# GpSimd in place of VectorE for the low parts of h and x in a split-precision feed-forward kernel

## The chip, the cores and the metric

The kernel runs on one core of one Trainium2 chip. The metric is device time in microseconds (us) of one execution, the median of several. The engines are named as the profile names them: PE is TensorE (matmuls), PEld its weight loads, DVE is VectorE, ACT is ScalarE, POOL is GpSimd and SP is SyncE, which issues all the DMAs here.

## What is computed

A gated linear attention runs over 4 batches, 8 heads, 768 steps and a head size of 48. Its output, laid out as 3072 tokens by 384, goes through a feed-forward layer with a squared ReLU (384 to 2048 to 384). The part of the reference that matters:

```python
for t in range(S):
    state = alpha[:, :, t, :, None] * state + np.einsum('bhd,bhe->bhde', k[:, :, t], v[:, :, t])
    y[:, :, t] = np.einsum('bhd,bhde->bhe', q[:, :, t], state)
x = y.transpose(0, 2, 1, 3).reshape(B * S, H * D)
h = np.maximum(x @ w_in, 0.0)
out = h * h @ w_out
```

## The kernel before

The attention is cut into 24 blocks (4 batches times 6 chunks of 128 steps). Four blocks make one group of 512 tokens, so there are six groups, 0 to 5. While the attention of one group is computed, the feed-forward layer of the group before it runs on TensorE; the two are woven together in program order.

For each group the feed-forward layer has an *input pass* (x times w_in, 16 tiles of h, each 128 features by 512 tokens) and an *output pass* (h squared times w_out, summed over the 16 tiles for four blocks of 128 tokens). Group 0's input pass and parts of the first output passes work with plain 32-bit matmuls. All else uses a faster matmul type with fewer bits (`fp32r`), and makes up for the lost bits by splitting every operand into parts:

- the *high part* `a` is a rounded copy of the tile, made by ScalarE (L596, tiles `ha`, `hx`, `xa`),
- the *low part* `l` is the tile minus its high part (L597, through the helper `combine`, so that the profile shows it under L547; tiles `hl`, `hx`, `xl`),
- the *difference* `d` is the low part minus 2^-12 times the high part, made by VectorE (L600, tiles `hd`, `xd`).

The weights are split in the same way (`wb`, `wl`, `wd`, L549 to L573), once, and the parts are kept in DRAM and streamed back for later groups. The product is then a sum of three matmul series: high with high (`a`, `b`), low with low (`l`, `l`), and difference with difference (`d`, `d`). In the input pass (L622) they are called for each tile j of h: the three matmuls with `xa`, the three with `xl`, and two tiles later the three with `xd`. In the output pass (L701) `out_x` first goes through the tiles n of h, and for each through four blocks: `ha` with `wb`, then `hl` with `wl`, eight matmuls a tile. Only after that `out_y` goes through the differences `hd` with `wd`.

h itself is made from the sums in PSUM by ScalarE and VectorE (L636 to L660); its square on VectorE is L651 or an L547 `hid<-hid`.

The order on every engine is the program order: the pool runs under a manual schedule, and `weave` (L923) places the attention's steps and the splits between the feed-forward units by costs and due times that are written in the table `AT`. In groups 2 to 5 the first three tiles of h are split already during the input pass (`AHEAD`). The other thirteen are split in the output pass, up to six tiles ahead of TensorE (`ahead`); the four named `hx` use tiles of the pool `raw`, in which x and its parts lie, the rest tiles of the pool `two` (22 buffers). Group 1 splits eight tiles of h, since the rest of its output pass is plain; group 0 splits four.

The low part of x is made in `split_x` (L609), three tiles of 128x512 in each of groups 1 to 5, ahead of the group's input pass.

GpSimd does the setting of zeros and of constants in the first 6 us. Later its queue holds only twelve empty instructions (`passed`, L456): one for each part of the attention's output products. [...]

The function around the change:

Of the kernel before, what the change touches and what calls it, by code (L numbers as in the profile page):

```python
# [9 lines left out]
FP32 = mybir.dt.float32  # L10
# [3 lines left out]
ALU = mybir.AluOpType  # L14
# [11 lines left out]
def kernel(  # L26
# [12 lines left out]
    nc = tc.nc  # L39
# [505 lines left out]
    def combine(steps):  # L545
        for o, x, op, z in steps:
            nc.vector.tensor_tensor(out=o, in0=x, in1=z, op=op)  # L547
# [46 lines left out]

    def split_to(a, l, x):
        nc.scalar.activation(out=a, in_=x, func=AF.Copy, scale=NEAR)  # L596
        combine(((l, x, ALU.subtract, a.bitcast(FP32)),))  # L597

    def diff_to(d, a, l):
        nc.vector.scalar_tensor_tensor(  # L600
# [8 lines left out]
    def split_x(g, kk):  # L609
        if kk == 0:  # L610
            x_parts["x"], x_parts["a"], x_parts["l"] = xT.pop(g), raw_r("xa"), raw_r("xl")
        split_to(x_parts["a"][:, kk], x_parts["l"][:, kk], x_parts["x"][kk])
# [68 lines left out]
    def split_h(n, i):  # L681
        r = i % (AHEAD + MORE)
        if r < AHEAD:
            a, l = two_k("ha", FP32R), two_k("hl", FP32R)
        else:
            if i == AHEAD:
                extra[:] = [raw_r("hx") for _ in range(3)]
            x = 2 * (r - AHEAD)
            a, l = (extra[y // 3][:, y % 3] for y in (x, x + 1))
        split_to(a, l, hid.pop(n))  # L690
        h_parts[n] = a, l
# [338 lines left out]
```

## Time and profile before

| what | value |
|---|---|
| three timed runs | 522.41, 522.62 and 522.86 us; median 522.62 |
| span of the profiled execution | 520.6 us from its first to its last instruction |
| what the median has beyond that span | 2.0 us |
| VectorE, 128x512 subtraction of `hl`, `hx`, `xl` | 40, 36 and 15 of them, mean 688, 685 and 688 ns |
| VectorE, difference `hd`, `xd` (L600) | 76 and 15, mean 692 and 685 ns |
| ScalarE, high part `ha`, `hx`, `xa` (L596) | 40, 36 and 15, mean 639, 618 and 640 ns |
| granted TensorE clock | 1.00 over the whole span |

The profile comes from one execution, whose own time beside its span was not taken down; the three runs are other executions. In a group's line the text behind the count is the busy time in us, the mean of one in ns, and then the engine's idle time ahead of the group with what ended it. A line of the timeline has the start, the length, the engine, the line of the code and the tiles, written as output<-inputs. PE's busy time is modelled, and its matmuls overlap, so that a busy TensorE isn't always one at its peak. Spans on POOL are rough.

### The profile page before, as it was taken

What the parts mean: (1) busy time and instruction counts of PE and PEld (TensorE: products, weight loads), DVE (VectorE), ACT (ScalarE), POOL (GpSimd) and SP (SyncE); (2) the same over time, 40 slices, a digit from 0 to 9 for tenths busy, and PEclk for the clock granted to TensorE, in tenths of its full rate; (3) what the DMA queues carried; (4) which work ended last, traced back from release to release, by engine and by line L of the source; (5) the groups of instructions that cost most, each with busy time, mean ns of one, the idle gap of its engine ahead of it and who ended that gap; (6) DMA issues with size and microseconds to landing.
All of it is one profiled execution on the core that took longest, in us unless ns stands there. A gap on an engine that the chain in (4) does not pass through costs nothing.

```text
span 520.6 us, 12925 instructions
## 1 busy us (share of the span) xinstructions
PE 510.8 (98%) x5276; PEld 418.2 (80%) x5276; DVE 366.0 (70%) x631; ACT 313.0 (60%) x650; POOL 5.4 (1%) x29
## 2 busy tenths in 40 slices
PE   7989999999999999999999999999999999999997
PEld 4754455668887668988899988899988899988997
DVE  4798989979978787867597476587465476363861
ACT  4668785677888594575963275963275763164620
POOL 4000000000000000000000000000000000000000
PEclk9999999999999999999999999999999999999999
DMA  9999687244686787898884788964673534898201
GB/s 161 209 278 213 196 240 218 60 114 176 224 200 196 195 246 198 264 317 206 195 248 148 251 246 198 230 187 150 231 255 126 179 126 151 268 340 293 70 0 62
DMA packets 140995, 102.36 MB, mean 197 GB/s; under 512 B 111476, under 2 KB 114568, under 8 KB 140936
## 3 DMA queue, kind: packets, MB, share of 16 engines
q1 hardware_dynamic: 140936, 101.53, 68.3%
q8 instruction: 42, 0.69, 0.6%
q14 instruction: 17, 0.14, 0.1%
HBM read 84.18 MB, written 17.33 MB: 195 GB/s over the span
## 4 chain that ended last, share of the span: by engine, by line
PE 93%; DVE 2%; SPq 2%; DMA 1%; issue 1%; POOL 1%; ACT 0%; POOLq 0%; DVEq 0%
PE o L701 41%; PE h L622 32%; PE h L805 7%; PE y L352 4%; PE T L482 2%; PE sckv L372 2%; PE sckv L395 2%; PE cs L265 1%; DMA qk_lent<-in_q_dram 1%; SPq L303 1%; SPq L109 1%; PE cs L268 1%; PE cs L269 1%; DVE x L515 0%; DVE w_in L182 0%
## 5 line engine op out<-in xcount | busy, mean ns | idle before, releaser
L622 PE MATMUL h<-xa,wb 128*128 128x512 f32 x240 | 68.2, 392 | 0.0
L622 PE MATMUL h<-xl,wl 128*128 128x512 f32 x240 | 67.9, 391 | 0.0
L622 PE MATMUL h<-xd,wd 128*128 128x512 f32 x240 | 67.3, 396 | 0.0
L515 ACT COPY x<-y 32x256 f32<-32x256 f32 (+2 forms) x132 | 47.2, 366 | 25.4 <-PE y L352 20.1
L547 DVE TENSOR_TENSOR hid<-h,hid 128x512 f32<-128x512 f32 x40 | 27.6, 689 | 45.5 <-PE h L622 45.4
L701 PE MATMUL o<-wb,ha 128*128 128x384 f32 x160 | 54.6, 342 | 0.0
L701 PE MATMUL o<-w_out,hid 128*128 128x384 f32 x160 | 54.0, 491 | 0.0
L701 PE MATMUL o<-wd,hd 128*128 128x384 f32 x304 | 53.8, 334 | 0.0
L701 PE MATMUL o<-wl,hl 128*128 128x384 f32 x160 | 53.5, 335 | 0.0
L639 ACT ACTIVATE h<-h 128x512 f32<-128x512 f32 x40 | 23.3, 582 | 49.7 <-PE h L622 49.7
L622 PEld LDWEIGHTS h<-xl,wl 128*128 128x128 f32 x240 | 45.1, 188 | 10.0 <-DVE xl L547 0.4
L701 PEld LDWEIGHTS o<-wd,hd 128*128 128x128 f32 x304 | 52.7, 188 | 0.3 <-DVE osb L737 0.3
L622 PEld LDWEIGHTS h<-xa,wb 128*128 128x128 f32 x240 | 44.6, 188 | 9.3 <-ACT xa L596 0.2
L622 PEld LDWEIGHTS h<-xd,wd 128*128 128x128 f32 x240 | 44.2, 188 | 9.2
L701 PE MATMUL o<-wb,hx 128*128 128x384 f32 x144 | 48.7, 338 | 0.0
L701 PE MATMUL o<-wl,hx 128*128 128x384 f32 x144 | 48.1, 334 | 0.0
L701 PEld LDWEIGHTS o<-w_out,hid 128*128 128x128 f32 x160 | 29.8, 190 | 19.3
L637 ACT ACTIVATE hid<-h 128x512 f32<-128x512 f32 x40 | 24.0, 600 | 34.6 <-PE h L622 34.5
L805 PE MATMUL h<-x,w_in 128*128 128x512 f32 (+1 forms) x108 | 43.6, 552 | 1.2 <-ACT x L515 1.2
L596 ACT ACTIVATE ha<-hid 128x512 fp32r<-128x512 f32 x40 | 25.6, 639 | 25.5 <-DVE hx L547 16.1
L805 PEld LDWEIGHTS h<-x,w_in 128*128 128x128 f32 x108 | 19.9, 190 | 21.1 <-issue 17.2
L547 DVE TENSOR_TENSOR hl<-hid,ha 128x512 fp32r<-128x512 f32 x40 | 27.5, 688 | 10.1 <-ACT ha L596 10.1
(114 smaller groups left out, 879.7 us busy)
## 6 DMA issues: line engine op xcount, KB each, us to landing
wd<-do SPq DMA_DIRECT2D x36, 384.0 KB, 3.7
wl<-lo SPq DMA_DIRECT2D x34, 384.0 KB, 4.0
wl<-li SPq DMA_DIRECT2D x32, 384.0 KB, 3.5
wd<-di SPq DMA_DIRECT2D x32, 384.0 KB, 3.9
raw<-in_moe_w_in_dram SPq DMA_DIRECT2D x8, 768.0 KB, 5.6
raw<-in_moe_w_out_dram SPq DMA_DIRECT2D x8, 768.0 KB, 5.6
v_in<-in_v_dram SPq DMA_DIRECT2D x24, 192.0 KB, 4.7
out_dram<-osb SPq DMA_DIRECT2D x24, 192.0 KB, 1.9
```

Source lines behind the costliest of these rows:

```text
L352: ins = nc.tensor.matmul(out=ys[e][64 * half : 64 * half + D + G * e, m % 2, p // 2, t], lhsT=lhsT, rhs=rhs, start=(half, e) not in seen, ...
L372: nc.tensor.matmul(out=ps[e][HALF[h], 0, p, :], lhsT=ks[rows, p, HALF[h]], rhs=qs[rows, p, HALF[h]], start=True, stop=True, skip_group_che ...
L395: nc.tensor.matmul(out=ps[h][64 * e : 64 * (e + 1), 1, p, G:64], lhsT=tile_of("k", n)[HALF[h], 2 * p + e, :], rhs=tiles["v"][n % NV][HALF[ ...
L482: nc.tensor.transpose(out=ps[h][:, i, p, :], in_=rows[HALF[h], 128 * p : 128 * (p + 1)], identity=ident[HALF[h], HALF[h]],)
L515: copy(out=x[kk][to : to + m, t : t + 2], in_=blk[n]["y"][e][r : r + m, :, p // 2],)
L547: nc.vector.tensor_tensor(out=o, in0=x, in1=z, op=op)
L596: nc.scalar.activation(out=a, in_=x, func=AF.Copy, scale=NEAR)
L622: nc.tensor.matmul(out=acc["h", j], lhsT=here[w, "i", p][:, kk, jj * 128 : (jj + 1) * 128], rhs=x_parts[x][:, kk], start=start and kk == 0 ...
L637: nc.scalar.activation(out=hid[j], in_=x, func=AF.Copy, scale=E)
L639: nc.scalar.activation(out=x, in_=x, func=AF.Copy, scale=1.0 + E)
L701: nc.tensor.matmul(out=acc[t][:, 0:DM], lhsT=lhs[:, t * C : (t + 1) * C], rhs=rhs, start=start, stop=stop, skip_group_check=True,)
L805: nc.tensor.matmul(out=ps, lhsT=w[:, kk, c0 : c0 + 128], rhs=xT[g][kk][:, cols], start=(kk == 0), stop=(kk == KM - 1),)
```

## The change

One line: the subtraction in `split_to`, which `split_x` and `split_h` call, is issued on GpSimd. Its operands, its place in the program and the buffers stay. The high part stays on ScalarE, the difference on VectorE, and the weights' subtractions (L561, L572) stay on VectorE.

```diff
     def split_to(a, l, x):
         nc.scalar.activation(out=a, in_=x, func=AF.Copy, scale=NEAR)
-        combine(((l, x, ALU.subtract, a.bitcast(FP32)),))
+        nc.gpsimd.tensor_tensor(out=l, in0=x, in1=a.bitcast(FP32), op=ALU.subtract)
```

76 subtractions of h and 15 of x, all 128x512, change their engine. In the program the calls of `split_to` stand behind those of `ga` that come earlier in the woven order, and so do the subtractions behind the empty instructions of L456 in GpSimd's queue.

## The prediction

> **What bounds the kernel.** First the busy times and the chain of work that ended last, on the page of before.
>
> ```profile
> PE 510.8 (98%) x5276; PEld 418.2 (80%) x5276; DVE 366.0 (70%) x631; ACT 313.0 (60%) x650; POOL 5.4 (1%) x29
> ...
> PE 93%; DVE 2%; SPq 2%; DMA 1%; issue 1%; POOL 1%; ACT 0%; POOLq 0%; DVEq 0%
> ```
>
> TensorE sets the time. Of its 9.8 us idle nearly all lies at the two ends; the stretches that I summed from 60 to 505.6 us (all but 212 to 217) show 0.96 us idle at 203 us, put down to "issue", and 0.04 us more. So relieving VectorE can win almost nothing, and what counts is whether TensorE must wait for a low part. The groups, kept apart by shape, give the prices:
>
> ```profile
> L547 DVE TENSOR_TENSOR hl<-hid,ha 128x512 fp32r<-128x512 f32 x40 | 27.5, 688 | 10.1 <-ACT ha L596 10.1
> L257 DVE TENSOR_TENSOR lo<-a_in,hi 128x384 fp32r<-128x384 f32 x16 | 8.9, 559 | 0.6
> L256 DVE CAST hi<-a_in 128x384 fp32r<-128x384 f32 x16 | 5.7, 355 | 6.5 <-ACT a_in L244 6.5
> L208 POOL COPY halves_mask<-causal 64x64 f32<-64x64 f32 x2 | 0.5, 234 | 0.1
> L204 POOL CAST causal_r<-causal 128x128 fp32r<-128x128 f32 x1 | 0.3, 291 | 0.1
> ```
>
> The margin is read from the timeline of the last group (VectorE alone), where the output pass begins and ends:
>
> ```profile
> 484.48 0.68 DVE L547 TENSOR_TENSOR hid<-hid 128x512 f32<-128x512 f32 x1
> 485.08 0.69 DVE L547 TENSOR_TENSOR hx<-hid,hx 128x512 fp32r<-128x512 f32 x1
> 485.87 0.69 DVE L600 SCALAR_TENSOR_TENSOR hd<-hx 128x512 fp32r<-128x512 f32 x1
> 486.48 0.68 DVE L547 TENSOR_TENSOR hx<-hid,hx 128x512 fp32r<-128x512 f32 x1
> ...
> 502.19 0.69 DVE L547 TENSOR_TENSOR hl<-hid,ha 128x512 fp32r<-128x512 f32 x1
> ```
>
> and TensorE's weight loads in the same stretch, the first that reads the low part of h tile 3 and the first that reads that of tile 15:
>
> ```profile
> 487.79 0.19 PEld L701 LDWEIGHTS o<-wl,hx 128*128 128x128 f32 x1
> ...
> 504.43 0.19 PEld L701 LDWEIGHTS o<-wl,hl 128*128 128x128 f32 x1
> ```
>
> Tile 3 is ready at 485.77, 2.0 us ahead of its load; tile 15 at 502.88, 1.6 us ahead. TensorE takes (504.43 - 487.79) / 12 = 1.39 us a tile (8 matmuls), VectorE a subtraction and a difference (`hd`, L600), some 1.40 us from start to start. Both run level, and the margin is thin. The same reading, tile 15: 1.9 us in groups 2 and 4 (281.55 to 282.23 against a load at 284.09; 435.77 to 436.46 against 438.45), 2.8 in group 3. Group 1 has only five such tiles, with 3.6 to 9.6 us, and group 0 four with 1.9 to 6.2.
>
> The low part of x has no margin in group 1. VectorE's three subtractions, and the weight load that waits for the third:
>
> ```profile
> 126.95 1.90 DVE L547 TENSOR_TENSOR xl<-x,xa 128x512 fp32r<-128x512 f32 x3 [0.92 <-ACT xa L596]
> ...
> 128.90 0.19 PEld L622 LDWEIGHTS h<-xl,wl 128*128 128x128 f32 x1 [0.36 <-DVE xl L547]
> ```
>
> In groups 2 to 5 `xl` is ready 2.7 to 9.5 us ahead.
>
> **Removed and added.** 91 subtractions of 128x512 (76 of h, 15 of x) leave VectorE's queue, 62 us by 0.69, and stand in GpSimd's, which after 6.2 us held nothing but the twelve empty instructions of L456. TensorE's, ScalarE's and SyncE's orders stay. The difference `hd` or `xd` now waits for another engine; behind it on VectorE stand the squares of h (L651), the attention steps and later differences. The first need of `hd` is 3.1 to 56 us after it is made (tile 15 of group 5: 503.60 against 508.25), so that wait alone costs nothing.
>
> GpSimd's price is not in the trace. Its two reading rows give (291 - 234) / 64 = 0.89 ns per element over a fixed 177 ns (two different operations, so a rough slope): 177 + 512 x 0.89 = 633 ns if both inputs come at once, 177 + 2 x 456 = 1089 ns if they take turns, 2 x 633 = 1266 ns at most by these rows. I take 1.09: VectorE's rows L256 and L257, same size, show that the second input costs (355 against 559 ns), and I see no reason for GpSimd to hide it. [...]
>
> Can GpSimd read while VectorE runs an operation with two SBUF inputs? No row shows the two together. The bounds are nothing (side by side) and the whole of VectorE's operation (one at a time). VectorE's rows fit two read paths: with two inputs 559, 688 and some 952 ns at 384, 512 and 768 elements are about 1.02 ns an element over 166; with one SBUF input 355 ns at 384 is (355 - 166) / 384 = 0.49, twice the rate. An operation with two inputs then fills both paths, so I take exclusion as the likelier end, well short of sure. [...]
>
> **The sum under exclusion.** Subtraction and difference take turns: 1.09 + 0.69 + 0.07 (a hand-over; VectorE's own is 0.03 to 0.10 us, 0.72 to 0.79 from a subtraction to its difference) = 1.85 us a tile, 0.46 over TensorE's 1.39. The first two subtractions go back to back, since `hd` must first hear of its own.
>
> Group 5: the square at 484.48 ends at 485.16; tiles 3, 4, a difference and 5 end at 485.16 + 3 x 1.09 + 0.69 + 0.1 = 489.2. Tile 5's load stands at 487.79 + 2 x 1.39 = 490.57, so 1.3 us are left; ten tiles at 0.46 take 4.6 and the square of L651 among them 0.7: TensorE is 4.0 us late.
>
> Groups 2, 3, 4: the empty instruction that ends part of the attention keeps GpSimd until TensorE is past it (261.5, 340.7, 416.8), no later than about where VectorE starts now. The same count puts the end of tile 8 at 273.2, 351.2 and 427.0 (one square each, in group 2 also L421), 1.2, 2.4 and 1.7 us ahead of its loads at 274.39, 353.57, 428.74; seven more tiles take 3.2. Late by 2.0, 0.8 and 1.5.
>
> Group 1's x: `xl` ends at 128.0, 129.2 and, with one `xd` (0.69) between, 131.0 against 128.90: 2.1 us. Groups 0 and 1 of h: nothing.
>
> Sum 4.0 + 2.0 + 0.8 + 1.5 + 2.1 = 10.4 us on a span of 520.6, so 531.0. The runs' median 522.62 lies 2.0 above that span, what is around it; I forecast **533.0**. If VectorE holds the path only for the 0.60 us from one start to the next (484.48 to 485.08), a tile takes 1.69, 0.30 over, and the same count gives 2.1 + 0.6 + 0 + 0.2 + 1.9 = 4.8 us, 527. At 1.27 us each of groups 2 to 5 loses 13 x 0.18 = 2.3 more and x 0.5: 20 us, 543. What is late next, `hd`, has 4.6 us or more in these groups and follows its subtraction by one turn.
>
> A second cover is the empty instruction itself: TensorE waits for it before the second half of the attention products (L469), and it now stands behind subtractions. In group 1 five are ahead of it; by the same count they end near 203.4, and the products stand at 207.3. If GpSimd ran 4 us further behind, that would cost too.
>
> **Rivals.** (a) Side by side at 1.09: GpSimd needs less than 1.39 a tile, so h costs nothing; only x does, 126.95 + 3 x 1.09 + 0.1 = 130.3 against 128.9, 1.4 us: 524.0. For it: GpSimd may have its own path. (b) Exclusion, but GpSimd's queue goes first whenever it has work: the low parts keep up, the differences pile up. From 485.16, 13 x 1.09 + 14 x 0.69 = 23.8 us end at 509.0 against 508.25 for the last difference, 0.8 late; with x's 1.4, 524.8. Against it: a difference that already waits would have to be passed over each time. (c) Not slower: side by side at the one-input price 0.63. Up to about 0.69 a subtraction, x in group 1 comes no later than now, and above it every 0.1 us costs 0.3 there. Nothing is lost, time 522.6; VectorE's relief could remove some of the short waits of TensorE's loads for q, k and weights products (0.2 to 0.8 us each, mostly hidden), at most about 1 us: 521.6. Against it: TensorE's row without gaps, and L257 against L256. (d) The price is above 1.27 with exclusion: over 543. That the change does nothing is out: the subtractions do stand in GpSimd's queue.
>
> **Numbers.** A measurement here tells 0.2%, about 1 us, from no change. Exclusion in turns 0.55 (527 to 543); (a) 0.17, of which 0.07 within 0.2%; (b) 0.12, 0.02 within; (c) 0.10, 0.06 within and 0.04 faster; (d) 0.06. Slower 0.55 + 0.10 + 0.10 + 0.06 = 0.81, same 0.15, faster 0.04. The range 523.2 to 543 leaves out (c) and (d).
>
> **What would show it.** The group `hl` on POOL near 1.1 us, or stretched toward 1.8 if blocked time counts as its own; `hd` starting only when no subtraction runs; L701 weight loads with idle time put down to POOL `hl` and `hx`, most in the last group; L622 with some 2 us put down to `xl`. Full-length overlap of POOL `hx` with DVE `hd` would make exclusion wrong, and a GpSimd price off 1.09 moves the sum by about 0.5 us per 0.01.

## The result, and the profile after

The changed kernel takes 528.96 us (median of four runs, 528.38 to 530.46) against 522.73 us for the kernel before in the same comparison: a ratio of 1.0119, 95% interval 1.0107 to 1.0132, some 6.2 us slower. The forecast was 533.0, within 523.2 to 543. The profiled execution took 529.03 us, its span is 527.3 us, 6.7 us longer than before's.

Busy times and the chain of the page of after:

```profile
PE 514.2 (98%) x5276; PEld 417.8 (79%) x5276; DVE 371.2 (70%) x540; ACT 312.3 (59%) x650; POOL 142.9 (27%) x120
...
PE 89%; DVE 3%; ACT 2%; SPq 2%; DMA 2%; issue 1%; POOL 1%; DVEq 0%; ACTq 0%
```

VectorE has 91 instructions fewer and is busy *longer*, 371.2 us against 366.0; GpSimd is busy 142.9 us with 91 more. Three groups of before, kept apart by shape, and then five of after say why:

```profile
L600 DVE SCALAR_TENSOR_TENSOR hd<-hx 128x512 fp32r<-128x512 f32 x36 | 24.9, 692 | 2.8 <-PE y L352 0.5
...
L701 PEld LDWEIGHTS o<-wl,hl 128*128 128x128 f32 x160 | 30.0, 188 | 0.3
...
L701 PEld LDWEIGHTS o<-wl,hx 128*128 128x128 f32 x144 | 27.0, 188 | 0.0
```

```profile
L600 DVE SCALAR_TENSOR_TENSOR hd<-hx 128x512 fp32r<-128x512 f32 x36 | 61.7, 1771 | 5.8 <-POOL hx L597 5.8
L597 POOL TENSOR_TENSOR hl<-hid,ha 128x512 fp32r<-128x512 f32 x40 | 59.9, 1503 | 236.0 <-ACT ha L596 231.7 <-DVE s L420 3.5 <-PE o L701 0.3
L597 POOL TENSOR_TENSOR hx<-hid,hx 128x512 fp32r<-128x512 f32 x36 | 56.8, 1609 | 105.4 <-ACT hx L596 34.0 <-DVE s L420 26.5 <-DVE hid L547 26.4
...
L701 PEld LDWEIGHTS o<-wl,hl 128*128 128x128 f32 x160 | 30.0, 188 | 2.3 <-POOL hl L597 2.0
L701 PEld LDWEIGHTS o<-wl,hx 128*128 128x128 f32 x144 | 27.0, 188 | 1.6 <-POOL hx L597 1.6
```

The difference from `hx` takes 1771 ns on the mean, with 692 before, though its own operands and shape stayed. The subtraction takes 1281 ns at the least (`hx`, by the view of that tile), 1733 at the median. And TensorE's loads of `hl` and `hx`, idle for 0.3 us in all before, now wait 3.6 us for GpSimd. In the last output pass the timeline of GpSimd and that of VectorE read:

```profile
489.53 6.25 POOL L597 TENSOR_TENSOR hx<-hid,hx 128x512 fp32r<-128x512 f32 x4 [18.59 <-issue]
495.74 5.13 POOL L597 TENSOR_TENSOR hl<-hid,ha 128x512 fp32r<-128x512 f32 x3
500.84 6.83 POOL L597 TENSOR_TENSOR hx<-hid,hx 128x512 fp32r<-128x512 f32 x4
507.62 3.43 POOL L597 TENSOR_TENSOR hl<-hid,ha 128x512 fp32r<-128x512 f32 x2
```

```profile
504.75 6.86 DVE L600 SCALAR_TENSOR_TENSOR hd<-hx 128x512 fp32r<-128x512 f32 x4
```

Both engines stand without a gap, overlapped, and neither moves faster than the other: (6.83 - 1.73) / 3 = 1.70 us from start to start on both. TensorE needs a tile every 1.39 us, so the margin shrinks by 0.31 a tile. From tile 10 on it is gone, and then the first load of a low part waits in every tile (TensorE's loads, tile 14 and tile 15):

```profile
509.42 0.19 PEld L701 LDWEIGHTS o<-wl,hl 128*128 128x128 f32 x1 [0.36 <-POOL hl L597]
...
511.11 0.19 PEld L701 LDWEIGHTS o<-wl,hl 128*128 128x128 f32 x1 [0.33 <-POOL hl L597]
```

The x of group 1, the loads of the second and third low part:

```profile
130.18 0.19 PEld L622 LDWEIGHTS h<-xl,wl 128*128 128x128 f32 x1 [0.86 <-POOL xl L597]
131.85 0.19 PEld L622 LDWEIGHTS h<-xl,wl 128*128 128x128 f32 x1 [1.48 <-POOL xl L597]
```

Setting the two traces' weight loads side by side, the k-th of a kind against the k-th, gives where the span grew:

| place | later by, us | forecast |
|---|---|---|
| first 60 us, where nothing changed (-0.1 to +1.0 in the other profiles) | 0.5 | - |
| group 0, the output tile (L737) | 0.4 | 0 |
| group 1, x | 2.1 | 2.1 |
| group 1, near 204 us | 0.5 | 0 |
| group 2, output pass | 0.6 | 2.0 |
| group 3 | 0.0 | 0.8 |
| group 4 | 0.8 | 1.5 |
| group 5 | 1.8 | 4.0 |
| sum | 6.7 | 10.4 |

The sum is the spans' difference, 6.7 us.

### The profile page after: what moved, and what is told of

Same layout as the page of the kernel before. It is cut to its first block, busy times and chain, and to the rows that moved or that the text cites. A ratio compares the mean times of both kernels' runs of the same rounds, so it can differ in the third digit from the quotient of the medians.

```text
span 527.3 us, 13045 instructions
## 1 busy us (share of the span) xinstructions
PE 514.2 (98%) x5276; PEld 417.8 (79%) x5276; DVE 371.2 (70%) x540; ACT 312.3 (59%) x650; POOL 142.9 (27%) x120
## 4 chain that ended last, share of the span: by engine, by line
PE 89%; DVE 3%; ACT 2%; SPq 2%; DMA 2%; issue 1%; POOL 1%; DVEq 0%; ACTq 0%
PE o L701 38%; PE h L622 32%; PE h L805 7%; PE y L352 4%; PE T L482 2%; PE sckv L372 2%; PE sckv L395 2%; DMA qk_lent<-in_q_dram 1%; PE cs L265 1%; ACT x L515 1%; SPq L303 1%; SPq L109 1%; POOL xl L597 1%; DMA a_in<-in_alpha_dram 1%; PE cs L268 1%
## 5 line engine op out<-in xcount | busy, mean ns | idle before, releaser
L597 POOL TENSOR_TENSOR hl<-hid,ha 128x512 fp32r<-128x512 f32 x40 | 59.9, 1503 | 236.0 <-ACT ha L596 231.7
L597 POOL TENSOR_TENSOR hx<-hid,hx 128x512 fp32r<-128x512 f32 x36 | 56.8, 1609 | 105.4 <-ACT hx L596 34.0
L600 DVE SCALAR_TENSOR_TENSOR hd<-hx 128x512 fp32r<-128x512 f32 x36 | 61.7, 1771 | 5.8 <-POOL hx L597 5.8
L600 DVE SCALAR_TENSOR_TENSOR hd<-ha,hl 128x512 fp32r<-128x512 f32 x40 | 38.9, 985 | 27.0 <-POOL hl L597 27.0
```

Of the source, the lines that this page charges most:

```text
L597: nc.gpsimd.tensor_tensor(out=l, in0=x, in1=a.bitcast(FP32), op=ALU.subtract)
L600: nc.vector.scalar_tensor_tensor(out=d, in0=a.bitcast(FP32), scalar=-E, in1=l.bitcast(FP32), op0=ALU.mult, op1=ALU.add)
```

## The experiments

**Do the two engines keep each other out?** Theory T says they take turns, rivals S and O that they share, or that GpSimd is just slow here. `m1_pairs` has nothing of the feed-forward layer; a stage is a loop of this kind (shortened: the output tiles take turns):

```python
for j in range(12):
    nc.gpsimd.tensor_tensor(out=p, in0=g[:, 0:512], in1=other[:, 0:512], op=ALU.subtract)
    nc.vector.scalar_tensor_tensor(out=o[:, 0:n], in0=g[:, 0:n], scalar=-0.5, in1=other[:, 0:n], op0=ALU.mult, op1=ALU.add)
```

> A kernel of its own that computes nothing of the reference: fifteen stages, each with 12 operations on GpSimd, on VectorE or on both, all independent of each other; a stage begins when both engines have ended the one before. Theory T (turns): a GpSimd operation that reads SBUF and a VectorE operation with two SBUF inputs keep each other out, one after the other, but each only for the time in which it moves data, and what is fixed in one (dispatch) hides in the other's turn. From the changed kernel's output pass: GpSimd about 1.15 us, VectorE about 0.55 us for 512 elements, so a pair takes 1.70 us from start to start on BOTH engines, against 1.25 to 1.28 and 0.60 alone. With VectorE's operation at 256 elements a pair takes about 1.42, at 1024 about 2.2, still one for one. With one SBUF input and one PSUM input, or with a fill, neither is slowed (1.25 and 0.60). With a GpSimd fill (writes only) VectorE keeps 0.60; with a GpSimd copy they take turns. Rival S (shared bandwidth): both run at once, slowed; VectorE isn't held to GpSimd's count and ends its 12 in about half to two thirds of GpSimd's time, at 256 elements in about half of that again. Rival O (no conflict; 1.7 us is the price of GpSimd's subtraction in this kernel): together as alone, VectorE 0.60, GpSimd 1.25 or 1.7 in both stages.

First GpSimd's twelve subtractions alone and VectorE's twelve operations beside GpSimd's fills, then both in the stage with 512 elements each (the part from 42 to 55 us):

```profile
3.79 14.69 POOL L57 TENSOR_TENSOR p_out<-gate,other 128x512 fp32r<-128x512 f32 x12 [1.60 <-DVE gate L48]
```

```profile
150.54 7.31 DVE L67 SCALAR_TENSOR_TENSOR v_out<-gate,other 128x512 f32<-128x512 f32 x12 [1.17 <-ACT gate L93]
```

```profile
41.19 14.87 POOL L57 TENSOR_TENSOR p_out<-gate,other 128x512 fp32r<-128x512 f32 x9 [0.74 <-ACT gate L93]
```

```profile
41.52 15.08 DVE L67 SCALAR_TENSOR_TENSOR v_out<-gate,other 128x512 f32<-128x512 f32 x9
```

Nine for nine, though alone VectorE would have done nine in 5.4 us. From the starts in the trace, median from start to start in us (VectorE's 0.60 is that beside GpSimd's fills, which is also its spacing in the kernel before; VectorE's stage without GpSimd ran on into GpSimd's next subtractions):

| GpSimd | VectorE | alone | together, both the same unless told |
|---|---|---|---|
| subtraction, 512 | two SBUF inputs, 512 | 1.22; 0.60 | 1.667 |
| subtraction, 512 | two SBUF inputs, 256 | 1.22; 0.336 | 1.400 |
| subtraction, 512 | two SBUF inputs, 1024 | 1.22; 1.135 | 2.200 |
| subtraction, 512 | copy, one SBUF input, 512 | 1.22; 0.336 | 1.400 |
| subtraction, 512 | PSUM and SBUF input, 512 | 1.22; 0.598 | 1.228 and 0.598 |
| copy, 512 | two SBUF inputs, 512 | 0.559; 0.60 | 1.015 |
| fill | two SBUF inputs, 512 | - ; 0.60 | VectorE 0.602 |

Beside a VectorE fill, GpSimd's subtraction kept 1.22. The first three rows lie on one line: 1.133 us + 1.04 ns for each of VectorE's elements (0.267, 0.533, 1.067). So T holds: one after the other, one for one, and a pair takes less than the two alone (1.667 us against 1.22 + 0.60). Read by this line, a turn is shorter than its instruction, 1.13 us of GpSimd's 1.26 and 0.53 of VectorE's 0.68; that the 1.13 is GpSimd's alone is inferred, and that a turn is the time in which data moves, as T has it, is my reading and was not shown. S is out, since VectorE is held to GpSimd's count, and O is out. The turns are no fixed rule: one GpSimd copy, at 156.17 us, took 2.15 us instead of 0.61 while VectorE started two more operations, and the runs don't show why.

**Without VectorE's two inputs in the pass.**

```diff
         h_diff[n] = two_k("hd", FP32R)
-        diff_to(h_diff[n], *h_parts[n])
+        nc.vector.memset(h_diff[n].bitcast(FP32), 0.0)
```

> As the changed kernel, but VectorE fills the differences hd with zeros (an operation of the same size without an input) in place of computing them, so that no VectorE operation with two SBUF inputs stands against GpSimd in the output pass, but for two squares; the difference's share of the output is left out. Theory T: GpSimd's subtractions of the pass fall from 1.70 to about 1.25 us from start to start, under TensorE's 1.39 us a tile, the losses of groups 2 to 5 (3.2 us) vanish, x's stays: 525 to 525.8 us. Rival O (GpSimd is slow by itself beside TensorE, ScalarE and the DMAs): 1.70 stays and so does 529 us.

Measured 525.99 us, ratio 1.0065 (1.0050 to 1.0079). The group `hx`, with 1.6 us on the mean in after:

```profile
L597 POOL TENSOR_TENSOR hx<-hid,hx 128x512 fp32r<-128x512 f32 x36 | 49.4, 1405 | 105.3 <-ACT hx L596 34.1 <-DVE s L420 26.5 <-DVE hid L547 26.4
```

In its last pass the subtractions stand 1.25 us apart, TensorE waits for none, and the margin grows from 1.5 us at tile 3 to 2.6 at tile 15. The fill still waits for GpSimd as the difference did (L695, 45 us of idle time put down to POOL `hl` and `hx`); what it lacks is the two inputs. T holds in the kernel too. The median lies above the expected 525.8 because three of the six runs, 526.53 to 527.25 us, had the half clock that comes below; the other three took 524.71 to 525.46.

**Which subtractions cost?** Four kernels move only some of them:

```diff
-    def split_to(a, l, x):
+    def split_to(a, l, x, pool=True):
         nc.scalar.activation(out=a, in_=x, func=AF.Copy, scale=NEAR)
-        nc.gpsimd.tensor_tensor(out=l, in0=x, in1=a.bitcast(FP32), op=ALU.subtract)
+        sub = nc.gpsimd if pool else nc.vector
+        sub.tensor_tensor(out=l, in0=x, in1=a.bitcast(FP32), op=ALU.subtract)
```

with `pool` true for x alone (e1), for h alone (e2), for the 24 with a wide margin (e4: x where `g > 1`, h where `n == i and i < AHEAD`), and for group 1's x alone (e5: `g == 1`).

> Only the 15 subtractions of x on GpSimd, those of h back on VectorE. Theory T with margins (only what has no margin costs): group 1's x alone has none; in the changed kernel the low part of its third tile came 1.9 us later against the matmuls ahead of it. So 522.7 + 1.9 = 524.6 us, up to 525.2. Rival E (each subtraction on GpSimd costs something, wherever it stands): 15/91 of 6.2 us, 523.7.

> Only the 76 subtractions of h on GpSimd, those of x back on VectorE. Theory T with margins: the output passes' losses of the changed kernel, 0.6 + 0 + 0.8 + 1.8 us in groups 2 to 5, and some 0.6 us in group 0, where TensorE waited for an output tile on VectorE: 526.0 to 526.6 us. Rival E (even): 76/91 of 6.2 us, 527.9.

> On GpSimd only the 24 subtractions that have a wide margin: the 12 of x in groups 2 to 5 (2.7 us and more) and the 12 of h that are split during the input pass of groups 2 to 5 (20 us and more). Theory T with margins: nothing, 522.7 us. Rival E (even): 24/91 of 6.2 us, 524.3.

> On GpSimd only the three subtractions of x in group 1. Theory T with margins: the whole of x's loss, as with all of x on GpSimd, 524.6 to 525.2 us. Rival E (even): 3/91 of 6.2 us, 522.9.

| kernel | median, us | ratio, 95% interval |
|---|---|---|
| e1, x | 526.84 | 1.0080 (1.0068 to 1.0092) |
| e2, h | 527.16 | 1.0087 (1.0074 to 1.0100) |
| e4, wide margin | 522.64 | 1.0004 (0.9995 to 1.0013) |
| e5, group 1's x | 526.18 | 1.0065 (1.0051 to 1.0078) |

Rival E falls: 24 subtractions cost nothing (e4), three cost 3.7 us (e5). But e1 and e5 overshoot T's 525.2, and 4.4 + 4.7 us for x and h alone are more than the 6.2 of both. T's own part is there: in the traces x costs 2.1 to 2.3 us by its waits, and the passes of groups 2 to 5 in e2 lose 0.6, 0.0, 0.7 and 1.8 us as expected. In e2 a further 0.9 us comes from an attention step, VectorE's scaling of q (0.55 us before), kept out by a subtraction of `hl`, and the transposes' load behind it (the timelines of VectorE and of TensorE's loads):

```profile
231.50 1.63 DVE L284 TENSOR_TENSOR q_in<-q_in,b 128x384 f32<-128x384 f32 x1
```

```profile
233.19 0.33 PEld L482 LDWEIGHTS T<-ident,q_in 64*128 64x128 f32 x8 [0.84 <-DVE q_in L284]
```

**A second price of a wait.** In e1, e3 and e5 the profile's clock falls to half for 3.41 us right behind x's waits. Busy times in e5, first the 3.41 us with the waits and then the next 3.41 us (the length, the busy time of PE, PEld, DVE, ACT and POOL with the number of instructions, then the granted clock PEclk, the DMA engines' share and GB/s):

```profile
127.56:130.97 3.41, 1.74 (x6) 0.74 (x5) 2.69 (x2) 1.08 (x2) 3.41 (x3) 1.00 0.30 115
130.97:134.38 3.41, 3.18 (x8) 2.51 (x9) 3.41 (x6) 0.58 (x1) 0.17 (x1) 0.50 0.24 87
```

TensorE is busy 1.74 of 3.41 us, 0.51, and runs the next stretch at half clock, which makes it about 1.3 to 1.6 us later still (1.3 between the two sorts of runs of e9 below; 1.6 between the traces of e9 and after, in which TensorE falls 4.1 and 2.5 us behind over group 0's output tile and x together). To see whether this hangs on the length of the wait, two kernels leave one or two of group 1's x on GpSimd (`pool = g == 1 and kk == 2`, and `kk >= 1`), and the change itself was run again.

> On GpSimd only one subtraction, the third of x in group 1. Theory T: it starts when VectorE's second one lets it in (128.2 us in the profile of before) and ends at about 129.4 instead of 128.85, so 0.5 us are lost: 523.0 us. Theory C (a second price: where TensorE is busy for only about half of a 3.41 us stretch, its clock is granted at half speed over the next 3.41 us, some 1.5 us more): with so short a wait never, the mean clock stays at 1.000 and the runs lie close together. Rival to C (any wait of TensorE here can bring the half clock): some runs 1.5 us longer at a mean clock of 0.997.

> On GpSimd the second and third subtractions of x in group 1. Theory T: they end at about 128.8 and 130.0 us, 0.5 and 1.1 to 1.3 late: 523.6 to 523.9 us. Theory C: TensorE stays busy for some 0.65 of the 3.41 us stretch, so no half clock: no run at 0.997 or below, no jump; with all three on GpSimd the runs were at 524.98 with a full clock and 526.2 to 526.8 with the half-clock stretch. Rival to C: runs at 0.997 here too, 525.2 us.

> The changed kernel once more, for its spread. Theory C: the stretches of 3.41 us do not start with the kernel, so the waits for group 1's x fall in one stretch or on two. The changed kernel's first profile had a stretch 0.54 busy and no half clock; at 0.51 busy and below it came in other kernels. So the runs fall in two sorts, 528.4 to 529.1 us at a full clock and about 530.4 at 0.997. Rival (the half clock belongs to kernels with x alone on GpSimd): all runs at 1.000, 528.4 to 529.1 us.

e7: 523.37 us, 1.0016 (1.0007 to 1.0025), 0.4 above the forecast, all runs at a mean clock of 1.000. e8: 524.77 us, 1.0042 (1.0030 to 1.0055), 0.999 or 1.000 in all runs; it is 0.9 us above the top of what was expected. In its trace x makes TensorE 1.6 us late and not 1.1 to 1.3, since a difference `xd` took a turn ahead of the third subtraction; that is 0.3 to 0.5 of the 0.9, and the rest is open (the profiled run took 524.15). e5, with three subtractions: 524.98 and 525.92 us at 1.000 and 0.999, and 526.18 to 526.79 at 0.995 to 0.997. e9: median 529.29 us, 1.0122 (1.0106 to 1.0137), of 528.25 and 528.81 at 0.999, 529.77 and 529.97 at 0.996; the kernel's first four runs had one at 0.997, 530.46. Both rivals to theory C fall, and the change as such falls in two sorts. The same pair of stretches in e9, then that with the waits in after, whose profile had no half clock, and in e8:

```profile
128.06:131.47 3.41, 1.82 (x8) 0.98 (x7) 2.99 (x2) 0.78 (x2) 3.29 (x3) 1.00 0.30 115
131.47:134.89 3.42, 3.42 (x8) 2.71 (x9) 3.42 (x7) 0.71 (x2) 0.00 (x0) 0.50 0.33 119
```

```profile
128.41:131.83 3.42, 1.85 (x8) 1.01 (x6) 2.91 (x2) 0.88 (x2) 3.39 (x3) 1.00 0.30 115
```

```profile
128.36:131.78 3.42, 2.13 (x8) 1.20 (x8) 3.42 (x4) 0.97 (x2) 2.18 (x2) 1.00 0.30 115
```

1.82 busy of 3.41 us brought the half clock, 1.85 did not, though the two profiles have the same two waits of TensorE's loads (0.86 and 1.48 us): the stretch began elsewhere. The changed kernel's own two profiles stand at 0.53 with the half clock and at 0.54 without it. That the deciding share is that of such a stretch is read from seven profiles (0.44, 0.47, 0.51, 0.51 and 0.53 with the half clock, 0.54 and 0.62 without it) and is a correlation: no run sets the share by itself. Busy times of PE are modelled, so the figure is rough.

**Every second tile.** `pool = n % 2 == 1` for h, x on VectorE.

> On GpSimd only the odd tiles of h, x on VectorE. Theory T (turns): two tiles take one GpSimd turn of 1.15 us and three VectorE turns of 0.60, 2.95 us, against TensorE's 2.78; over six pairs that is 1.0 us, within the margin of 1.5 to 2.8 us that before has at the end of each pass: 522.7 to 523.3 us. Rival: an operation on GpSimd keeps VectorE out for its whole length, 1.28 + 3 x 0.69 = 3.35 us for two tiles, 0.57 over; 3.4 us less the margin, 1.9 us in group 5, 1.5 in 2 and 4: 526 to 528 us.

Measured 530.08 us, 1.0138 (1.0117 to 1.0159): half the moves don't save half the loss. Three of its four runs have the half clock (0.996 and 0.997); the fourth, 527.84 us at 0.999, is somewhat faster than the whole change at that clock (528.25 to 529.03), so that it is worse than the whole change isn't shown. Theory T's 523.3 is missed either way. The fourth run lies in the rival's range, but the rival's whole-length exclusion falls with `m1_pairs`. VectorE, and TensorE's load of tile 10's low part, in the last pass:

```profile
500.75 1.77 DVE L601 SCALAR_TENSOR_TENSOR hd<-ha,hl 128x512 fp32r<-128x512 f32 x1 [1.18 <-POOL hl L598]
502.44 1.75 DVE L598 TENSOR_TENSOR hx<-hid,hx 128x512 fp32r<-128x512 f32 x1
```

```profile
504.24 0.19 PEld L702 LDWEIGHTS o<-wl,hx 128*128 128x128 f32 x1 [2.13 <-DVE hx L598]
```

VectorE's subtraction of tile 10 stands in its queue behind the difference of tile 9, which waits 1.18 us for GpSimd, and then both share turns with GpSimd's next. In the full change no subtraction of h stands in that queue, and the differences there are not needed soon. My count had the turns and not the queue. This is read from the trace; no run isolates it. A stretch 0.47 busy and the half clock follow here too.

## Why the prediction was right

**Exclusion in turns, the forecast: right.** It was the likelier end, taken from two rows of VectorE; `m1_pairs` and e3 show it. Rival (a) falls with them, (b) because in the kernel's last pass the two engines keep the same pace (four operations in 6.83 us on GpSimd, four in 6.86 on VectorE), (c) by the time and the price. The condition of (d), a price above 1.27, was nearly met (1.26 to 1.28), but its time, over 543, did not come. The time alone would have decided little: the range 523.2 to 543 held (a) and (b) as well, at 524.0 and 524.8.

**The size of a turn: too large, the term that was mis-sized.** I took 1.09 + 0.69 + 0.07 = 1.85 us a tile; it is 1.70 in the kernel and 1.67 in `m1_pairs`. Two errors work against each other. GpSimd's price was too low: 1.26 to 1.28 at least in the kernel, 1.26 alone, at the top of my ends of 0.63 and 1.27. But whole durations must not be added: by the line above, 1.13 + 0.53 count. That the forecast came within 4 us is in part luck: with the true price the same sum gives 543. The second case of the prediction, 1.69 a tile and 527, has the right turn and nearly the right losses, but from 1.09 + 0.60 in place of 1.13 + 0.53, so again by errors that cancel.

An excess of 0.31 in place of 0.46 makes of group 5's ten tiles 3.1 us in place of 4.6. The 0.7 us for the square of L651 did not come at all, since the square took one turn as a difference does (1.78 us at 497.94 in after, against 1771 ns on the mean for `hd`). The 1.3 us of margin at tile 5 were right, and 3.1 - 1.3 = 1.8 us is what was measured. Groups 2 to 4 lost less too, which is not worked out tile by tile; 8.3 us of forecast for the output passes became 3.2.

**x in group 1: right by its wait**, 2.1 us, in the forecast order (two subtractions, a difference, the third). What it left out is the half clock, 1.3 to 1.6 us in some runs.

**"That wait alone costs nothing": incomplete.** The differences are not needed soon, as forecast. But what stands behind them on VectorE waits too, other two-input operations are kept out as well (the scaling of q in e2, 1.63 us instead of 0.55), and some are needed at once. In group 0 a difference waits 1.17 us for GpSimd, the subtraction of a weight's part behind it is kept out, and both put off the output tile that TensorE waits for (before, then after):

```profile
118.90 0.95 DVE L547 TENSOR_TENSOR wl<-w_in,wb 128x768 fp32r<-128x768 f32 x1
...
124.09 1.94 DVE L737 SCALAR_TENSOR_TENSOR osb<-o,osb 128x384 f32<-128x384 f32 x4
```

```profile
118.53 0.69 DVE L600 SCALAR_TENSOR_TENSOR hd<-ha,hl 128x512 fp32r<-128x512 f32 x1 [1.17 <-POOL hl L597]
...
120.00 2.03 DVE L547 TENSOR_TENSOR wl<-w_in,wb 128x768 fp32r<-128x768 f32 x1
...
125.17 1.94 DVE L737 SCALAR_TENSOR_TENSOR osb<-o,osb 128x384 f32<-128x384 f32 x4
```

The weight's subtraction takes 2.03 us (0.95 before), and the output tiles start at 125.17 instead of 124.09, 0.5 us of which come from the first 60 us; TensorE's loads wait 0.9 us for them, of which 0.4 stays. A loss near 204 us appears only with h on GpSimd (0.5 us in after, 0.2 in the same kernel's e9, 0.4 in e2, 0.3 in e6), but the profile names no releaser there; its cause is open.

**The empty instruction of L456: right.** It waits for a matmul of `ga` (L455), and one of `gb` (L469) for it; TensorE's loads wait 0.3 us for it in all, as before.

**What would show it: one sign was wrong.** I wrote that a full-length overlap of `hx` and `hd` in the profile would refute exclusion. They do overlap in full, and the recorded length grows, from 692 to 1771 ns at the same work; I read the growth as time for which the instruction is kept out and which counts as its own. Not the overlap but the stretched length tells it.

## What to carry to other kernels

Moving work from VectorE to GpSimd took nothing off VectorE here, where its other operations have two SBUF inputs (371.2 us busy against 366.0): add the two engines' turns, here 1.13 and 0.53 us, and compare that with what the consumer needs per tile, here 1.39. The same move cost nothing, and won nothing, where the margin is wide (e4, ratio 1.0004). Beside VectorE operations with one SBUF and one PSUM input neither engine was slowed in `m1_pairs` (1.228 us on GpSimd and 0.598 on VectorE, against 1.22 and 0.598 alone), and in after VectorE's `us<-sckv,s`, with `sckv` in PSUM, takes its 0.34 us inside a GpSimd subtraction (275.64 us). And a wait of the busiest engine can cost more than its length, when the clock falls behind it (1.3 to 1.6 us more here).

## What the runs showed of the hardware that I had not expected

The half clock (a granted clock of 0.50). Two waits of TensorE's loads close together, 0.86 and 1.48 us, were enough in e9 and not in after; in e6 a single one of 2.13 us stands ahead of it. In e1, e5 and e9 it lasts 3.41 us. The time at full clock before it is 126.29 us in e1 and e5, 37 times 3.413 us, and, as the clock's record has it, starts at another moment of the kernel in each (4.68 us in e5, 6.72 in e1). I read this as stretches of one length that lie elsewhere in each execution, which would be why the same kernel meets the half clock in some runs (two of four in e9).

A plain copy on VectorE with one SBUF input (0.336 us for 512 elements, alone) also takes turns with GpSimd's subtraction: together 1.400 us, as with 256 elements of two inputs.
